# Lending more tiles to VectorE's exp, partial waves, and a normalisation that goes through DMA, in a four-layer attention kernel

## The chip, the cores and the metric

The kernel runs on one core of a Trainium2 chip. The core has TensorE (PE, matrix products into PSUM), VectorE (DVE), ScalarE (ACT), GpSimd (POOL), SyncE (SP, which issues the DMAs here), an on-chip SBUF of 128 partitions and a PSUM of eight banks of 512 float columns. The metric is the device time of one execution in microseconds, median over the runs of one kernel; the median of the kernel before is 1751.68 us.

## The reference

Four attention layers run on one sequence of 2048 tokens with 512 features and 32 heads of 16. Layers 0 and 2 are of kind A, layers 1 and 3 of kind B, each with a residual:

```python
x = x + _A_ref(_layernorm(x), A_wq, A_wk, A_wv, A_wo, A_beta)
x = x + _B_ref(_layernorm(x), B_wqkv, B_wo)
x = x + _A_ref(_layernorm(x), A_wq, A_wk, A_wv, A_wo, A_beta)
x = x + _B_ref(_layernorm(x), B_wqkv, B_wo)
```

Kind A works on four segments of 512 tokens: causal attention within the segment, plus a linear memory, mixed by a gate per head:

```python
a_dot = softmax(qs @ ks.T * scale + mask) @ vs
num   = phi(qs) @ M
den   = phi(qs) @ z + 1e-6
o     = g * (num / den) + (1.0 - g) * a_dot
M, z  = M + phi(ks).T @ vs, z + sum(phi(ks))
```

with `g = sigmoid(beta)` and `phi(t) = t + 1` for `t > 0`, else `exp(t)`. Kind B is plain full attention, softmax(q kᵀ / 4) v over all 2048 tokens. In B every head needs 2048 x 2048 exps, in A about half of 512 x 512 for each segment.

## The kernel before

The program is written by a planner. `Builder` runs through the work once in Python, with a clock for each engine that it estimates itself (`Sched.t`), and each engine's list of instructions comes out in the order in which the planner emitted them. Semaphores join the lists. A table, `PIECES`, changes the planner's settings at given times of its clock.

The work is cut into *groups*: one layer, one segment of 512 queries, four heads (chunk `c` of eight heads, `e` the even or odd ones). A group of kind B has 64 *banks*: scores of 128 keys against 512 queries for one head, 512 columns of one PSUM bank. The whole kernel has 4,864 banks. In each step (`unit`) TensorE computes the scores of two or three banks with 32-row matmuls, four of which run side by side, and ScalarE takes the exp of all of them in one instruction into `pT` (L1707). Two or three units later TensorE multiplies the exps by V (`pv`) into the accumulating bank `ACC`. V carries a seventeenth column of ones for each head, so the product also holds the sum of the exps. For full groups of B, and all groups of layer 3, the product has 17 rows by 512 queries (`fm`); for A and for partial groups of layer 1 it is done by 128 queries at a time, 17 columns per head.

VectorE takes part of the exps off ScalarE. `dx_first` (L1248) reads a bank or two from PSUM and writes, in integer arithmetic, the bits of an approximate exp into a *slot*; `dx_shift` (L1318) adds a constant to a whole slot, once for each further *chord* of the approximation, and `pool_part` (L1363) does the same on GpSimd. Each of the chords is multiplied by V on TensorE, so that such a bank costs three or four products instead of one. Slots are the tiles `dxw` (two banks each) and, once they are free, tiles of other uses that lend their space (`dx_areas`, four banks each): before, the second slots of `QA` and `VA` from the end of layer 0 until `("proj", 2, 2)`, and in layer 3 the tiles that nothing needs any more. `dx_room` decides whether a bank may go to VectorE, from how far VectorE's planned clock runs ahead of the next unit.

When a group's last product is done, `finish` normalises it. For full groups of B (`finish_fm`) VectorE transposes the 128x512 sums in 32x32 blocks (L1840), inverts the sums of exps (L1843), multiplies (L1846), and after the pair `e = 0, 1` transposes back into `oT` (L1868), from which the output projection reads. For A the inverse is also multiplied by the gate `gout` (L1816). All else (layer norm, projections, the memory, the output projection) is done by *tasks*, which the planner fits between units. While TensorE would idle, `keep_busy` gives it products with a tile of zeros. SP issues the DMAs in order, and each waits there for its semaphores: loads, stores, and the 128x512 transposes of `xT`, `oT`, `phk` and `phq`.

Of the kernel before, what the change touches and what calls it, by code (L numbers as in the profile page):

```python
# [3 lines left out]
dt = mybir.dt  # L4
# [3 lines left out]
P = 128  # L8
# [23 lines left out]
class Op:  # L32
    __slots__ = ("eng", "idx", "fn", "deps", "emit", "evno", "is_dma", "batch", "name", "end", "ghost", "ready")
# [48 lines left out]
class Sched:  # L82
# [80 lines left out]

    def add(self, eng, fn, reads=(), writes=(), deps=(), name="", banks=(), ns=300, gap=None, tile=None, extra=None):
# [9 lines left out]
        for (bk, mode, alloc) in banks:  # L174
            if mode == "w":
                if bk.alloc != alloc:
                    tail = bk.writes[-1:] + list(bk.reads.values())
# [20 lines left out]
        wit = {}  # L198
        for w in [d for g in dep_ops if g.ghost for d in g.deps] + dep_ops:
            if w.eng == "pe" and eng == "pe" and not w.is_dma:  # L200
                continue
            if w.is_dma:
                wit[("dma", id(w.batch))] = w
                continue
            cur = wit.get(w.eng)
            if cur is None or cur.idx < w.idx:
                wit[w.eng] = w
        for w in wit.values():
            if not w.is_dma:
                w.emit = True  # L210
        op.deps = list(wit.values())
        if eng == "pe" and extra is None and self.idle is not None:
            ready = max([d.end + LAG[d.eng] for d in op.deps if d.eng != "pe"], default=0.0)
            if name != "fill" and self.last:
                self.settle(ready)
            if ready > self.t["pe"] + 312:
                self.idle(ready, banks)
                op.idx = len(self.ops[eng])
                self.owed = 0
            elif self.owed and tile[0] == 128:  # L220
                self.idle(self.t["pe"], banks, self.owed)
                op.idx = len(self.ops[eng])
                self.owed = 0
        if extra is not None:
# [72 lines left out]
class Group:  # L297


    __slots__ = ("L", "kind", "qseg", "c", "e", "ksegs", "first", "last", "banks", "pos", "qm", "acc", "npv", "idx", "total", "started", "left", "taken", "shut", "fm")  # L300

    def __init__(self, L, kind, qseg, c, e, ksegs, first=True, last=True):
# [16 lines left out]
        self.idx = c * 2 + e  # L319
# [8 lines left out]
class Builder:  # L328
    NPU, NDX, FIT, MARGIN, PART, FILL_DVE, EARLY, FILL = 4, 5, 2, 450, 1, 300, 700, 0.5
# [7 lines left out]
    QREST, CLOSE, FM, NAREA, XDX, NEAR_S, NEAR_E, DX_WAIT = 24, ('proj', 2, 2), 3, 18, 99, 60, 60, 400  # L337
# [4 lines left out]
    PIECES = [(0.0, {'MIX': 0, 'OPART': 4}),  # L342
              (20.0, {'EVAC_ACT': -300, 'LOW': 32, 'DXA_REST': 14}),
              (60.0, {'CR_W': 1900, 'AHEAD': 500, 'LOW': 24, 'DXA_REST': 10, 'wide': True}),
              (100.0, {'DQ': 1900, 'wide': True}),
              (140.0, {'EVAC_ACT': 0, 'CR_W': 1400, 'AHEAD': 300, 'DX_T': 480, 'DQ': 2200}),
              (180.0, {'DX_FIN': 2500, 'PE_B': 5, 'PE_LOW': 5, 'DMA_LATE': 300}),
              (220.0, {'DX_FIN': 2000, 'PE_B': 4, 'PE_LOW': 6, 'LOW': 16, 'DX_T': 430, 'PVN': 6, 'DMA_LATE': 600}),
              (260.0, {'LOW': 24, 'NEAR_N': 200, 'PVN': 4, 'HOR': 100, 'DX_RES': 2}),
              (300.0, {'MARGIN': 700}),  # L350
              (340.0, {'FILLS': 1, 'DQ': 1900, 'DMA_LATE': 300, 'NEAR_E': 80}),
              (380.0, {'DX_T': 330, 'DQ': 2500, 'DMA_STEPS': 3, 'NEAR_E': 0, 'PSH_N': 16, 'PSH_E': 1}),
              (420.0, {'NEAR': 6}),
              (460.0, {'NEAR': 10, 'TAKEN': 1.5, 'ALTA': (1, 9, 9, 9), 'PSH': 1}),
              (480.0, {'REST': 14, 'REST_N': 20, 'PSH_E': 0, 'PSH_B': 6}),
# [623 lines left out]
    def task_B(self, L, s):  # L979
        ks = self.kslot(L, s)  # L980
        need = [("x", L, s)]
        if L == 3:
# [3 lines left out]
            if s == 2:  # L986
                need.append(("closed", self.CLOSE))
# [1102 lines left out]
```

## Time and profile before

| what | value |
|---|---|
| median of 3 runs | 1751.68 us (1751.64 to 1751.69) |
| span of the profiled execution, which is the only time given of it | 1749.6 us |
| ScalarE busy | 1708.2 us, 98% |
| TensorE busy | 1638.0 us, 94% (modelled ends) |
| VectorE busy | 1489.3 us, 85% |
| GpSimd busy | 650.2 us, 37% |
| DMA | 30.10 MB, 17 GB/s |

A row of a view of groups gives the line, the engine, the operation, the tile written and the tiles read, the shape and the count; then busy time in us, the mean duration in ns, and the engine's idle time just before such instructions with what ended it. The matmuls overlap, and so do the tails of neighbouring instructions on VectorE and ScalarE: count times mean is more than busy time.

### The profile page before, as it was taken

To read this page: it belongs to the slowest core of one execution; us is meant where nothing else is said; L and a number is where in the kernel's file an instruction comes from. 1 tells how busy PE (TensorE), PEld (TensorE's weight loads), DVE (VectorE), ACT (ScalarE), POOL (GpSimd) and SP (SyncE) were. 2 spreads that over 40 slices of the span, in tenths; PEclk is the share of its full clock that TensorE was granted. 3 is DMA by queue.
4 is the path that set the end of the run, shared out by engine and by line. 5 is a ranking of instruction groups with operands and counts; after the bars stand their busy time and mean duration, and the time that the engine had idled before them with its cause. 6 is when DMAs were issued, how large, how long until landed. Compare 5 with 4: busy or idle time off the path is not lost.

```text
span 1749.6 us, 44053 instructions
## 1 busy us (share of the span) xinstructions
PE 1638.0 (94%) x17651; PEld 574.8 (33%) x17651; DVE 1489.3 (85%) x2912; ACT 1708.2 (98%) x1662; POOL 650.2 (37%) x1204
## 2 busy tenths in 40 slices
PE   8989999999998999999999999999999999999998
PEld 4445454563224222233222332242222222222222
DVE  6677767589996999897999779767999999999997
ACT  7999999999999999999999999999999999999998
POOL 4632415110016212224221252151155556766665
PEclk9999999999999999999999999999999999999999
DMA  6121101000001000000001011010000000000000
GB/s 176 21 46 32 32 17 26 14 12 5 13 1 26 1 1 13 14 19 7 14 10 22 7 23 16 13 26 13 1 13 1 2 7 8 1 1 13 1 1 13
DMA packets 86189, 30.10 MB, mean 17 GB/s; under 512 B 78816, under 2 KB 85472, under 8 KB 85984
## 3 DMA queue, kind: packets, MB, share of 16 engines
q1 hardware_dynamic: 85984, 27.29, 7.5%
q8 instruction: 138, 2.26, 0.6%
q14 instruction: 67, 0.55, 0.1%
HBM read 6.30 MB, written 2.10 MB: 5 GB/s over the span
## 4 chain that ended last, share of the span: by engine, by line
ACT 45%; PE 30%; issue 13%; DVE 7%; POOL 2%; DMA 1%; SPq 0%; ACTq 0%; DVEq 0%; POOLq 0%
ACT pT L1707 44%; PE ps L563 30%; POOL pT L1722 2%; ACT amem L821 1%; DMA xT<-xn 1%; DVE KB L1248 1%; DVE dxw L1248 1%; DVE QA L1248 1%; DMA phk<-KA 0%; DVE xT L1248 0%; DVE dxw L1318 0%; DVE KA L1840 0%; DVE amem L946 0%; DVE VB L1248 0%; DVE VB L601 0%
## 5 line engine op out<-in xcount | busy, mean ns | idle before, releaser
L1707 ACT ACTIVATE pT<-ps 128x1024 bf16<-128x1024 f32 (+4 forms) x1612 | 1676.6, 1186 | 26.6 <-PE ps L563 19.7
L563 PE MATMUL ps<-qm,KB 32*128 32x512 bf16 x3584 | 526.0, 384 | 52.5 <-ACT pT L1707 39.0
L563 PE MATMUL ps<-pT,VB 128*17 128x512 bf16 x2187 | 371.5, 384 | 5.6 <-ACT pT L1707 2.3
L1722 POOL TENSOR_SCALAR_AFFINE_SELECT pT<-pT 128x256 bf16<-128x256 bf16 (+2 forms) x523 | 211.8, 416 | 220.7 <-ACT pT L1707 208.0
L563 PEld LDWEIGHTS ps<-qm,KB 32*128 32x128 bf16 x3584 | 134.0, 91 | 448.2 <-ACT pT L1707 336.8
L1363 POOL TENSOR_TENSOR dxw<-dxw,dxc 128x256 int32<-128x256 int32 (+1 forms) x127 | 77.7, 614 | 389.6 <-DVE dxw L1248 64.7
L563 PEld LDWEIGHTS ps<-pT,VB 128*17 128x17 bf16 x2187 | 86.6, 87 | 232.0 <-issue 199.2
L1248 DVE TENSOR_SCALAR dxw<-ps 128x512 uint16<-128x512 f32 (+1 forms) x232 | 158.5, 697 | 4.4 <-PE ps L563 3.2
L1617 POOL TENSOR_SCALAR qm<-QB,par 128x512 bf16<-128x512 bf16 x88 | 67.7, 776 | 245.6 <-PE ps L563 220.7
L1248 DVE TENSOR_SCALAR QA<-ps 128x512 uint16<-128x512 f32 (+1 forms) x170 | 120.7, 729 | 3.3 <-PE ps L563 2.8
L563 PE MATMUL ps<-qm,QA 32*128 32x512 bf16 x512 | 113.2, 384 | 8.9 <-ACT pT L1707 5.9
L563 PE MATMUL ps<-qm,KA 32*128 32x384 bf16 (+3 forms) x1024 | 101.8, 303 | 16.9 <-ACT pT L1707 13.1
L563 PE MATMUL ps<-dxw,VW 128*17 128x512 bf16 x472 | 117.5, 381 | 0.0
L563 PE MATMUL ps<-VA,pT 128*128 128x51 bf16 (+1 forms) x2560 | 105.6, 187 | 10.3 <-POOL pT L1722 6.5
L1248 DVE TENSOR_SCALAR VA<-ps 128x512 uint16<-128x512 f32 (+1 forms) x149 | 107.1, 733 | 4.4 <-PE ps L563 3.4
L1318 DVE TENSOR_SCALAR dxw<-dxw 128x1024 uint16<-128x1024 uint16 (+1 forms) x261 | 105.5, 414 | 3.4 <-PE ps L563 1.1
L563 PEld LDWEIGHTS ps<-VA,pT 128*128 128x128 bf16 x2560 | 83.7, 96 | 58.2 <-POOL pT L1722 26.1
L1248 DVE TENSOR_SCALAR KB<-ps 128x512 uint16<-128x512 f32 (+1 forms) x122 | 93.9, 787 | 4.5 <-PE ps L563 3.8
L563 PE MATMUL ps<-wB,zero 128*128 128x512 bf16 x271 | 90.4, 383 | 0.0
L563 PE MATMUL ps<-dxw,VB 128*17 128x512 bf16 x297 | 89.5, 382 | 0.1
L1248 DVE TENSOR_SCALAR VB<-ps 128x512 uint16<-128x512 f32 (+1 forms) x106 | 82.7, 794 | 3.6 <-PE ps L563 2.7
L563 PE MATMUL ps<-xT,wA 128*128 128x512 bf16 (+1 forms) x273 | 76.2, 381 | 1.3 <-DVE xT L782 0.9
(343 smaller groups left out, 2844.3 us busy)
## 6 DMA issues: line engine op xcount, KB each, us to landing
out_dram<-x SPq DMA_DIRECT2D x8, 256.0 KB, 2.1
x<-in_A_x_dram SPq DMA_DIRECT2D x3, 512.0 KB, 5.1
wB<-in_B_wqkv_dram SPq DMA_DIRECT2D x1, 1536.0 KB, 11.7
xT<-xn SPq DMA_TRANSPOSE x60, 2.4
oT<-ob SPq DMA_TRANSPOSE x36, 2.4
x<-in_A_x_dram SPq DMA_DIRECT2D x4, 128.0 KB, 2.4
wA<-in_A_wq_dram SPq DMA_DIRECT2D x1, 512.0 KB, 4.7
wA<-in_A_wk_dram SPq DMA_DIRECT2D x1, 512.0 KB, 5.8
```

Of the source, the lines that this page charges most:

```text
L563: self.sc.add("pe", lambda e: e.matmul(out, lhsT, rhs, start=start, stop=stop, skip_group_check=True), reads=reads, banks=[(bank, "w", all ...
L821: self.op("act", lambda e: e.activation(et, src, ACT.Exp), reads=bsrc, writes=self.b_amem, ns=1023, gap=915)
L1248: self.sc.add("dve", lambda e: e.tensor_scalar(d, o, SCALE * LOG2E * 128, W_C if dxs[0][:3] in self.wt else EXP_C, op0=ALU.mult, op1=ALU.add),
L1318: self.op("dve", lambda e: e.tensor_scalar(o, w, d, None, op0=ALU.add), reads=self.b_dxw[b0][:len(ents)], writes=wr, ns=(295, 425, 560, 69 ...
L1363: self.sc.add("pool", lambda e: e.tensor_tensor(o, w, c, ALU.add), reads=self.b_dxw[src][i0:i0 + n] + [self.b_dxc], writes=wr, deps=[sync] ...
L1617: self.op(eng, (lambda m, q, col: lambda e: e.tensor_scalar(m, q, col, 0.0, op0=ALU.mult, op1=ALU.add))(m, q, col), reads=[bq, self.b_par] ...
L1707: self.sc.add("act", (lambda dst, src: lambda e: e.activation(dst, src, ACT.Exp, scale=SCALE))(dst, src), writes=self.b_pT[slot * 3 + i:sl ...
L1722: self.op("pool", (lambda blk, pat: lambda e: e.affine_select(blk, blk, pattern=pat, compare_op=ALU.is_ge, fill=0.0, base=0, channel_multi ...
```

## The change

*More lenders.* `dx_areas` lists more tiles. In layer 0 the slots 2 and 3 of `KB`, `VB` and `QB` lend halves (two banks each) from the end of segment 0 until their own segment of layer 0 is done; `KB`, `VB` 4 and 5 and `QB` 0 to 2 lend in layer 2; `QB` 0 to 2 lend again in layer 3. A lender with an end is closed before the projection that writes it (`task_B` waits for `("closed", ...)`). `dxw` has four slots instead of five.

*Partial waves.* `early_parts` and `split_early` may start a pair of a B group with those key segments that are there, if the scores ahead are few (`EARLY_R`); the sums go to a free place (`accS`, slots 8 and up) and the rest of the group adds to them.

*Normalisation.* A full group's sums are only copied (or added) from PSUM to a tile `fin`. `den_rows` moves the sums of exps by DMA into a 128x32 tile `den`, VectorE inverts that once for a pair, `row` and `inv` bring the inverses through DRAM to a 128x512 tile, and GpSimd multiplies into `oT` (`run_norms`). The very last pair goes the old way.

*Gate.* V's ones column of A holds `1 + exp(beta)` instead of 1, so the sum of exps comes out already divided by `1 - g`; the product with `gout` goes, and the memory's denominator is adjusted with `gden`.

*Table.* `PIECES` is new, and `side` lets some small operations go to GpSimd where a setting says so. In the program that results none does: every `xn`, `Mn`, `Mz` and `oT<-oT,phq` still stands on VectorE.

```diff
-    NPU, NDX, FIT, MARGIN, PART, FILL_DVE, EARLY, FILL = 4, 5, 2, 450, 1, 300, 700, 0.5
+    NPU, NDX, FIT, MARGIN, PART, FILL_DVE, EARLY, FILL = 4, 4, 2, 450, 1, 300, 700, 0.5
...
-    PIECES = [(0.0, {'MIX': 0, 'OPART': 4}),
-              (20.0, {'EVAC_ACT': -300, 'LOW': 32, 'DXA_REST': 14}),
+    PIECES = [(0, {'MIX': 0, 'OPART': 4}),
+              (20, {'CR_LOW': 1500, 'DQ': 1900, 'PAIRS2': 0, 'DXS': 2, 'EVAC_ACT': -300, 'LOW': 32}),
...
+    def moves(self, pairs, reads, writes, key, ns=2450):
+
+        t = self.tsems[self.ring("tsem", 8)]
+        b, last = DmaBatch(t[0], t[1]), [t[2]] if t[2] is not None else []
+        for out, in_ in pairs:
+            t[1] += 16
+            t[2] = self.sc.add_dma("sp", (lambda out, in_: lambda e: e.dma_start(out, in_))(out, in_), b, reads=reads, writes=writes, deps=last, ns=ns,
+                                   gap=self.MOVE)
...
+        on = bcast(g[:, 0:1], [[0, 8], [1, H]])
+        self.op("dve", lambda e: e.tensor_copy(va[:, :, :, 16], on), reads=[self.b_gone], writes=[b for l in self.b_VA for b in l], ns=430)
...
+        for s in self.EARLY_S:
+            for t, b in ((self.KB, self.b_KB), (self.VB, self.b_VB), (self.QB, self.b_QB)):
+                add(t[:, s, :, :], b[s], ("attn", 0, 0), until=("attn", 0, s), halves=True)
+        for ks, s in ((4, 0), (5, 1))[:self.MORE]:
+            add(self.KB[:, ks, :, :], self.b_KB[ks], ("acc", 1), until=("attn", 2, s))
+            add(self.VB[:, ks, :, :], self.b_VB[ks], ("attn", 1, 0), until=("attn", 2, s))
+        for s in range(3 if self.MORE else 0):
+            add(self.QB[:, s, :, :], self.b_QB[s], ("attn", 1, s), until=("attn", 2, s))
...
+        for s in range(3 if self.MORE else 0):
+            add(self.QB[:, s, :, :], self.b_QB[s], ("attn", 3, s))
...
+            if pair is None and self.EARLY_Q and sum(len(g.banks) - g.pos for g in self.sel) <= self.EARLY_R:
+                pair = self.split_early()
...
+            if rows:
+                d = self.fin[g.e]
+                self.op("dve", lambda e: e.tensor_copy(d, acc), writes=self.b_fin[g.e] + new, bank=bank, alloc=g.acc, ns=690)
...
-            om = bcast(self.gout[:, h:h + 1], [[0, 4], [2, 4]])
-            r4 = rd.rearrange("p (t r) -> p t r", r=4)
-            self.op("dve", lambda e: e.tensor_tensor(r4, r4, om, ALU.mult), reads=[br, self.b_gout], writes=[br], ns=160)
...
+    def den_rows(self, g):
+
+        f, bf, c = self.fin[g.e], self.b_fin[g.e], self.den[:, :]
+        key = g.L, g.qseg, g.c
+        at = lambda a, o, dims: bass.AP(tensor=a.tensor, offset=a.offset + o, ap=dims)
+        w = f.ap[0][0]
+        self.moves([(at(c, 16 * g.e, [[32, P], [1, 16]]), at(f, 16 * w, [[32 * w, 4], [16, 32], [1, 16]]))], [bf[1]], [self.b_den[g.e]], ("den",) + key)
+        if g.e:
+            self.moves([(self.fin[0][32 * r + 16:32 * r + 32, :], f[32 * r:32 * r + 16, :]) for r in range(4)], [bf[0]], [self.b_fin[0][1]], ("fin",) + key)
+            self.norms.append([0, g])
+
+    def run_norms(self, now):
+
+        while self.norms:
+            stage, g = self.norms[0]
+            key = g.L, g.qseg, g.c
+            if not now and not self.met([("dma", ("inv" if stage else "den",) + key)]):
+                return
+            c = self.den[:, :]
+            if not stage:
+                self.op("dve", lambda e: e.reciprocal(c, c), reads=self.b_den, writes=self.b_den, ns=351)
+                at = lambda a, o, dims: bass.AP(tensor=a.tensor, offset=a.offset + o, ap=dims)
+                self.moves([(at(self.row, 512 * e, [[1024, 4], [16, 32], [1, 16]]), at(c, 16 * e, [[32, P], [1, 16]])) for e in range(2)], self.b_den,
+                           self.b_row, ("row",) + key)
+                self.moves([(self.inv[:, :], at(self.row, 0, [[512, 8], [0, 16], [1, 512]]))], self.b_row, [self.b_inv], ("inv",) + key, 3500)
+                self.norms[0][0] = 1
+                continue
+            self.norms.pop(0)
+            self.own(g)
+            o, f, v = self.oT[:, 1, g.c, :], self.fin[0], self.inv[:, :]
+            ns = (690, 1045)[self.INV_P]
+            op = self.op(("dve", "pool")[self.INV_P], lambda e: e.tensor_tensor(o, f, v, ALU.mult), reads=self.b_fin[0] + [self.b_inv],
+                         writes=[self.b_oT[1][g.c]], ns=ns)
```

How the lists change, at three places. On ScalarE in the last third of the program, where layer 2 ends and layer 3 runs, `pT<-ps` are the exps; 1536 columns are three banks, 1024 two. Before:

```order
L1707 ACTIVATE pT<-ps 128x1536
L1707 ACTIVATE pT<-ps 128x1024 x3
L1707 ACTIVATE pT<-ps 128x1536
L1707 ACTIVATE pT<-ps 128x1024 x2
L1707 ACTIVATE pT<-ps 128x1536 x2
```

and now:

```order
L1828 ACTIVATE pT<-ps 128x1024 x4
L1828 ACTIVATE pT<-ps 128x1536
L1828 ACTIVATE pT<-ps 128x1024 x10
L1828 ACTIVATE pT<-ps 128x1536
L1828 ACTIVATE pT<-ps 128x1024 x18
```

Nearly every unit there now leaves one or two of its banks to VectorE.

On VectorE in layer 3, at the end of a full group with `e = 1` (`KA` holds the tiles `tk`, `of` and now `fin`; the `TENSOR_SCALAR ...<-ps` are first exp steps, those of 2048 columns are later steps on a lent tile). Before:

```order
L1840 STREAM_TRANSPOSE KA<-ps 128x512
L1843 RECIPROCAL rd<-KA 128x16
L1846 TENSOR_TENSOR KA<-KA,rd 128x16x16
L1248 TENSOR_SCALAR xT<-ps 128x512
L1248 TENSOR_SCALAR phq<-ps 128x512
L1868 STREAM_TRANSPOSE oT<-KA 128x512
```

and now:

```order
L1922 COPY KA<-ps 128x512
L1325 TENSOR_SCALAR KA<-ps 128x512
L1325 TENSOR_SCALAR VA<-ps 128x1024
L1325 TENSOR_SCALAR VA<-ps 128x512 x2
L1977 RECIPROCAL den<-den 128x32
```

The two transposes and the product are gone; the reciprocal stands some exp steps behind the copy and waits for a DMA.

On SP during layer 1, with the tasks of layer 2 beside it. Before, only transposes stand there:

```order
L608 DMA_TRANSPOSE oT<-ob 128x4x128
L608 DMA_TRANSPOSE phk<-KA 128x4x128 x4
L608 DMA_TRANSPOSE oT<-ob 128x4x128 x3
L608 DMA_TRANSPOSE xT<-xn 128x4x128 x8
L608 DMA_TRANSPOSE oT<-ob 128x4x128
```

and now:

```order
L650 DMA den<-KA 128x1x16
L640 DMA_TRANSPOSE xT<-xn 128x4x128 x4
L650 DMA den<-KA 128x1x16
L650 DMA KA<-KA 16x512 x4
L650 DMA row<-den 4x32x16 x2
L650 DMA inv<-row 128x1x512
L640 DMA_TRANSPOSE xT<-xn 128x4x128 x4
```

The chain of a pair stands between two sets of transposes of normalised x; the second set can be issued only after `inv`, which waits for `row`.

More of the change, by code (lines that the diff above doesn't have):

```diff
@@ L223, in add @@
                 self.owed = 0
+        for w in op.deps:
+            if not w.is_dma:
+                w.emit = True
         if extra is not None:
```

421 lines of the change are left out of this document (261 added, 160 removed).

## The prediction

> **What bounds the kernel now.** I read the head of the page first, then the chain of waits, ScalarE's waits, and the busy time by stretch.
>
> ```profile
> span 1749.6 us, 44053 instructions
> PE 1638.0 (94%) x17651; PEld 574.8 (33%) x17651; DVE 1489.3 (85%) x2912; ACT 1708.2 (98%) x1662; POOL 650.2 (37%) x1204
> ACT 45%; PE 30%; issue 13%; DVE 7%; POOL 2%; DMA 1%; SPq 0%; ACTq 0%; DVEq 0%; POOLq 0%
> L1707 ACT ACTIVATE pT<-ps 128x1024 bf16<-128x1024 f32 (+4 forms) x1612 | 1676.6, 1186 | 26.6 <-PE ps L563 19.7
> ```
>
> ScalarE works 1708.2 of 1749.6 us, and 1676.6 us of that is one line, the exp of the scores (L1707). It idles 41.4 us in all, 26.6 of them before an exp. The chain alternates between ScalarE and TensorE, but that is a loop: TensorE waits for a bank that ScalarE must empty.
>
> ```profile
> 400.00:500.00 100.00, 96.25 (x843) 26.56 (x841) 97.77 (x192) 100.00 (x100) 7.70 (x11) 1.00 0.04 8
> 0.00:400.00 400.00, 369.02 (x5691) 201.39 (x5691) 286.12 (x677) 378.93 (x372) 134.98 (x322) 1.00 0.19 41
> 400.00:1350.00 950.00, 900.09 (x8490) 281.62 (x8488) 829.59 (x1665) 940.35 (x930) 267.25 (x525) 1.00 0.06 12
> 1350.00:1740.00 390.00, 363.35 (x3442) 90.41 (x3438) 369.80 (x561) 385.71 (x359) 248.00 (x358) 1.00 0.01 4
> ```
>
> Columns: stretch, its length, busy time (and instructions) of PE, weight load, DVE, ACT and POOL, then the granted clock. Of the 41.4 us of idle ScalarE, 21.1 lie in the first 400 us (loads and the first layer), 9.7 in the next 950 and 4.3 in the last 390. So the time is ScalarE's list of exps, and an edit is worth what it takes off that list. VectorE does some exps in its place. It has room early (286 of 400 us) and hardly any in the last layer (369.8 of 390).
>
> **The change on ScalarE.** I counted the instructions of both orders; the prices are these rows.
>
> ```profile
> L1707 ACT ACTIVATE pT<-ps 128x1024 bf16<-128x1024 f32 x873 | 855.9, 1079 | 8.8 <-PE ps L563 7.5 <-POOL pT L1722 0.6
> L1707 ACT ACTIVATE pT<-ps 128x1536 bf16<-128x1536 f32 x580 | 834.3, 1497 | 14.4 <-PE ps L563 10.0 <-POOL pT L1722 1.6 <-POOL qm L1617 0.3
> L599 ACT ACTIVATE KB<-ps 128x512 bf16<-128x512 f32 x3 | 1.9, 617 | 0.0
> ```
>
> Exps of 1536 columns go from 580 to 429, of 1024 from 873 to 1074; of the small ones, 512 wide go from 27 to 4, 2x256 from 28 to 8, 3x256 from 48 to 58, 256 from 56 to 66. That is 1,864,192 columns in 1612 instructions before and 1,826,304 in 1639 after: 37,888 columns, 74 score banks of 512, have left ScalarE. Two rows differ by 512 columns and 1497 - 1079 = 418 ns, so the columns save 74 x 0.418 = 30.9 us. At 0.418 us per 512, all columns of before are 1521.9 of the 1676.6 us; the other 154.7 us over 1612 instructions are 0.096 us each, and 27 more cost 2.6 us. Evacuations on ScalarE rise by 5: 5 x 0.6 = 3.0 us. Sum: -30.9 + 2.6 + 3.0 = **-25.3 us**.
>
> **The change on VectorE.** It must take the 74 banks.
>
> ```profile
> L1248 DVE TENSOR_SCALAR dxw<-ps 128x512 uint16<-128x512 f32 x226 | 151.2, 683 | 3.7 <-PE ps L563 2.6 <-POOL dxw L1363 0.4
> L1248 DVE TENSOR_SCALAR KB<-ps 128x1024 uint16<-128x1024 f32 x24 | 29.2, 1218 | 1.5 <-PE ps L563 1.0 <-POOL VB L1363 0.3
> L1318 DVE TENSOR_SCALAR dxw<-dxw 128x1024 uint16<-128x1024 uint16 x221 | 94.5, 436 | 2.9 <-PE ps L563 1.1 <-DVE QA L1248 0.2
> L1318 DVE TENSOR_SCALAR VA<-VA 128x2048 uint16<-128x2048 uint16 x47 | 32.6, 695 | 0.2 <-PE ps L563 0.2
> L1840 DVE STREAM_TRANSPOSE KA<-ps 128x512 f32<-128x512 f32 x47 | 33.2, 707 | 4.9 <-PE ps L563 4.6
> L1843 DVE RECIPROCAL rd<-KA 128x16 f32<-128x16 f32 x55 | 14.0, 254 | 1.9
> L1846 DVE TENSOR_TENSOR KA<-KA,rd 128x256 bf16<-128x256 f32 x55 | 23.4, 426 | 1.9
> L1868 DVE STREAM_TRANSPOSE oT<-KA 128x512 bf16<-128x512 bf16 x27 | 19.0, 703 | 0.2
> L1816 DVE TENSOR_TENSOR rd<-rd,gout 128x16 f32<-128x16 f32 x64 | 13.9, 217 | 2.2
> L1798 DVE COPY KB<-ps 128x512 f32<-128x512 f32 x4 | 2.7, 681 | 0.1
> L933 DVE RECIPROCAL rg<-rg 128x128 f32<-128x128 f32 x6 | 5.7, 953 | 0.2
> L1800 DVE TENSOR_TENSOR KB<-KB,ps 128x272 f32<-128x272 f32 x12 | 5.2, 431 | 0.6 <-PE ps L563 0.3
> ```
>
> First exp steps (L1248): 30 more of 512 and 22 more of 1024, 30 x 0.683 + 22 x 1.218 = +47.3. Later steps (L1318): 103 fewer of 1024 (-44.9), 49 more of 2048 (+34.1), 19 new of 1536, put halfway between 0.436 and 0.695 (+10.8): about 0. That is what the lent tiles buy: four banks go through one step at 0.174 us each instead of two at 0.218. The normalisation: 54 fewer each of the transpose, reciprocal and product, 54 x (0.707 + 0.254 + 0.426) = -74.9; 27 fewer output transposes, -19.0; 64 gate products, -13.9. In their place 40 copies of 0.681 (+27.2), 4 fewer 512-wide adds (-2.7), and 24 reciprocals of 32 columns, between the 254 ns of 16 and the 953 of 128, by width 0.35 each (+8.5). The partial waves add six copies, adds, reciprocals and products, 6 x (0.431 + 0.431 + 0.254 + 0.426) = +9.3; 5 fewer evacuations are -3.4. Sum: **-21 us** on an engine that had 260 us of idle. Over the kernel VectorE hides its work; where it may not is the first rival.
>
> **GpSimd and TensorE** stay under cover.
>
> ```profile
> L1363 POOL TENSOR_TENSOR dxw<-dxw,dxc 128x256 int32<-128x256 int32 x126 | 76.7, 611 | 388.2 <-DVE dxw L1248 64.7 <-PE ps L563 60.3 <-DVE xn L755 40.4
> L1363 POOL TENSOR_TENSOR VB<-KB,dxc 128x512 int32<-128x512 int32 x5 | 5.2, 1037 | 4.0 <-DVE KA L1846 1.5 <-PE ps L563 1.3 <-DVE VB L1318 0.6
> L563 PE MATMUL ps<-wB,zero 128*128 128x512 bf16 x271 | 90.4, 383 | 0.0
> L563 PE MATMUL ps<-pT,VB 128*17 128x512 bf16 x2187 | 371.5, 384 | 5.6 <-ACT pT L1707 2.3
> L563 PE MATMUL ps<-VB,pT 128*128 128x51 bf16 x1454 | 65.8, 187 | 0.1
> ```
>
> GpSimd gets 72 steps of 256 (+44.0), 15 of 512 (+15.6) and the 24 float products of 128x512; the nearest row, the integer add of that size, makes these 24 x 1.037 = +24.9. Some 650 + 85 = 735 us is 43% of the new span; without cover a late product would hold the next pair's sums, which come only after another 64 banks.
>
> TensorE loses 60 idle-time matmuls on zeros (60 x 90.4/271 = -20.0) and 450 products of probabilities and V in the 17-row form (at most 450 x 371.5/2187 = -76.4, at least 0 where they overlap others), and gains 2412 of the narrow form (2412 x 65.8/1454 = +109). It stays between +13 and +89 us busy, against 111.6 us idle plus the zeros that are left. The clock row reads 1.00 in the last 390 us too, where few zeros run, so fewer cost no clock.
>
> **The DMA chain.** Each of 24 pairs now sends, on SP's one queue, two `den`, four `KA<-KA`, two `row` and one `inv` (219 DMAs more with three extra transposes); `row` waits for VectorE's reciprocal and `inv` for `row`, with transposes of the next rows of x behind them.
>
> ```profile
> xT<-xn SPq DMA_TRANSPOSE x60, 2.4
> x<-in_A_x_dram SPq DMA_DIRECT2D x4, 128.0 KB, 2.4
> x<-in_A_x_dram SPq DMA_DIRECT2D x3, 512.0 KB, 5.1
> out_dram<-x SPq DMA_DIRECT2D x8, 256.0 KB, 2.1
> ```
>
> No row has these forms. From 2.1 us for a write to DRAM and between 2.4 and 5.1 us for the 256 KB of `inv`, the three hops are 6.6 to 9.6 us, with reciprocal and product 8 to 11. Cover: a pair's 128 banks take 128 x 390/1264 = 39 us in the last layer (1,264 is what its 1271 score matmuls in 390 us come to). I take the chain at nothing on the path.
>
> The Trainium skill, "DMA: Bandwidth & Descriptors", "Why a DMA increments its semaphore by 16 and not by 1", speaks against it: a DMA is spread over the largest number of engines up to 16 that divides the slowest dimension on both sides, which is 4 for `den` and `row` and 8 for `inv`. With that page's roughly 2 us fixed and 27 GiB/s per engine, `inv` would be about 3.1 us by my estimate, inside the bounds above; the sum stays as it is.
>
> **The sum.** 1749.6 - 25.3 = 1724.3 us if ScalarE's idle time stays. It may grow in the last layer. There (the last 1,264 banks by the orders) ScalarE's banks go from 849 to 817 and its exps from 363 to 390, which is 32 x 0.418 - 27 x 0.096 = 10.8 us of the gain. VectorE's list there gets about 7 us longer by the rows above: 369.8 + 7 = 376.8 us of work for a stretch of 390 - 10.8 = 379.2. The fullest window quoted has VectorE 97.77% busy; at that the stretch takes 385.4, and 6.2 us of the gain is lost. Nothing is lost if the denser list overlaps more: the 226 steps of 683 ns in the first row of VectorE make 154.4 us and cover only 151.2, since neighbours overlap. Between 0 and 6.2 I take 3.5, since the window had few GpSimd steps. Span: 1728. The runs lie 1751.7 - 1749.6 = 2.1 us above the span: **1730 us**, own range 1724 to 1737.
>
> **Rivals.** (1) VectorE becomes the bound in the last layer. For it: 95% busy there, and the same step takes different times depending on what runs beside it:
>
> ```profile
> L1318 DVE TENSOR_SCALAR dxw<-woA 128x1024 uint16<-128x1024 uint16 x4 | 1.7, 418 | 0.0
> L1318 DVE TENSOR_SCALAR dxw<-phk 128x1024 uint16<-128x1024 uint16 x6 | 3.0, 503 | 0.0
> ```
>
> If its 376.8 us must keep today's 94.8% share (369.8 of 390), the stretch takes 397.5 instead of 379.2 and the end is 1749.6 - 25.3 + 18.3 + 2.1 = 1745; range 1737 to 1748. Against it: a bank goes to VectorE only while its planned backlog is below a limit (`dx_room`), as before, and ScalarE then idled 4.3 us in 390.
>
> The Trainium skill, "SBUF — State Buffer", "SBUF: two separate sides", says that VectorE's fast two-port steps and GpSimd's work share a port pair, and whichever comes second waits for the whole instruction. The 85 ns between these two rows agree. By that rule the added GpSimd work makes this rival likelier.
>
> (2) The DMA chain costs time: VectorE's reciprocal stands in its list where the plan (2.45 us per hop) has the data landed. If `den` lands 1.3 us later than that and each of the 24 stalls reaches ScalarE, 31 us are lost: 1726.4 + 31 = 1757, slower; it decides from 1.2 us on. Against: the planned figure is already at the 2.4 us rows, VectorE has slack outside the last layer.
>
> (3) The early gain isn't delivered: partial waves and early lenders fill a list that is short of score work, ScalarE waits more in the first 400 us (21.1 idle now), and only the last layer is worth something: about 1751, no change.
>
> (4) Better: the partial waves close half of those 21.1 us: 1717 to 1723.
>
> **Chances.** Forecast 0.64, (1) 0.20, (2) 0.04, (3) 0.05, (4) 0.07. The range 1721 to 1744 leaves out (2), (3), some of (1) and (4). A measurement tells 0.2%, 3.5 us, from no change: faster 0.91, same 0.05, slower 0.04.
>
> **What would show it.** Right: L1707's counterpart near 1648 us, ScalarE's idle time 38 to 50 us, VectorE near 1470 busy and above 96% in the last layer, DMA waits of VectorE and PE of a few us in all. Wrong: ScalarE's idle time above 60 us. If it stands ahead of exps in the last layer with VectorE's first steps named by TensorE's waits, it is (1); with `den` as the releaser, (2); in the first 400 us, (3).

## The result, and the profile after

| | before | after |
|---|---|---|
| median of the runs | 1751.66 us (4 runs, 1751.25 to 1751.69) | 1736.42 us (4 runs, 1733.77 to 1738.21) |
| ratio, 95% interval | | 0.9911 (0.9897 to 0.9925) |
| profiled execution: span | 1749.6 us | 1732.0 us |

The change is faster by 15.2 us, 0.9%. The forecast was 1730 us with the range 1721 to 1744. Four more runs of the same kernel, with the experiments below, gave 1735.96 us and a ratio of 0.9901 (0.9881 to 0.9922). From the page of the changed kernel:

```profile
span 1732.0 us, 48101 instructions
PE 1596.1 (92%) x19355; PEld 625.5 (36%) x19553; DVE 1476.5 (85%) x2761; ACT 1681.6 (97%) x1694; POOL 742.4 (43%) x1317
ACT 40%; PE 27%; DVE 16%; issue 12%; POOL 2%; DMA 2%; SPq 0%; ACTq 0%; DVEq 0%; POOLq 0%
L1828 ACT ACTIVATE pT<-ps 128x1024 bf16<-128x1024 f32 (+3 forms) x1639 | 1648.7, 1154 | 37.1 <-PE ps L595 32.4
L1988 POOL TENSOR_TENSOR oT<-KA,inv 128x512 bf16<-128x512 f32 x24 | 32.7, 1362 | 114.2 <-DMA inv<-row 75.2
```

ScalarE's busy time fell from 1708.2 to 1681.6 us, by 26.6, where 25.3 were forecast; its exps (now L1828) take 1648.7 us. Its idle time rose from 41.4 to 1732.0 - 1681.6 = 50.4 us. So 26.6 us were gained and 9.0 given back: 17.6 us of span in these two executions. VectorE's share of the chain of waits went from 7% to 16%.

Where the 9 us lie is read from the busy time by stretch (columns as in the prediction; the fifth number is ScalarE). Before:

```profile
400.00:1230.00 830.00, 788.30 (x7521) 252.72 (x7518) 717.99 (x1473) 821.33 (x822) 218.97 (x454) 1.00 0.07 13
1230.00:1350.00 120.00, 111.80 (x969) 28.90 (x970) 111.60 (x193) 119.02 (x110) 48.28 (x71) 1.00 0.02 6
1350.00:1700.00 350.00, 326.79 (x3069) 81.20 (x3065) 333.41 (x509) 345.75 (x321) 220.05 (x319) 1.00 0.01 4
```

After:

```profile
0.00:400.00 400.00, 362.78 (x5938) 209.92 (x6009) 294.74 (x696) 380.23 (x378) 129.26 (x316) 0.99 0.19 40
400.00:1230.00 830.00, 767.11 (x8977) 294.36 (x9082) 701.14 (x1374) 818.14 (x818) 275.50 (x534) 1.00 0.10 19
1230.00:1350.00 120.00, 106.26 (x1002) 28.64 (x1010) 108.79 (x174) 113.33 (x119) 80.52 (x118) 1.00 0.09 25
1350.00:1700.00 350.00, 334.33 (x3228) 85.25 (x3240) 346.61 (x482) 344.78 (x359) 248.67 (x342) 1.00 0.06 16
```

ScalarE's idle time is 19.8 us in the first 400 us (21.1 before), 11.9 from 400 to 1230 (8.7), 6.7 from 1230 to 1350 (1.0) and 5.2 from 1350 to 1700 (4.3), although VectorE is 99% busy there. What grew most is the start of the last layer, not its bulk. One gap makes most of it. TensorE and ScalarE at that place, as start, duration, instruction and wait:

```profile
1333.88 1.04 PE L595 MATMUL ps<-woB,oT 128*128 128x512 bf16 x4
1335.78 1.04 PE L595 MATMUL ps<-woB,oT 128*128 128x512 bf16 x4 [0.86 <-DVE x L1102]
1337.60 1.04 PE L595 MATMUL ps<-woB,oT 128*128 128x512 bf16 x4 [0.78 <-DVE x L1102]
```

```profile
1339.06 1.02 ACT L1828 ACTIVATE pT<-ps 128x1024 bf16<-128x1024 f32 x1 [4.30 <-PE ps L595]
1340.71 1.02 ACT L1828 ACTIVATE pT<-ps 128x1024 bf16<-128x1024 f32 x1 [0.63 <-PE ps L595]
```

These matmuls are the output projection of segment 0, three of its four tiles in one row, without a score between them, each waiting for VectorE to empty the one bank they share. The planner put them there in `own`: a pair's product may be written to `oT` only when the segment that still owns that place has been projected, and the next pair's end (`run_norms(True)` in `finish`) asked for the product at once. That is read from the code and these rows; no run moves the projection.

### The profile page after: what moved, and what is told of

It reads as the page before. It is cut to its first block, busy times and chain, and to the rows that moved or that the text cites. A ratio compares the mean times of both kernels' runs of the same rounds, so it can differ in the third digit from the quotient of the medians.

```text
span 1732.0 us, 48101 instructions
## 1 busy us (share of the span) xinstructions
PE 1596.1 (92%) x19355; PEld 625.5 (36%) x19553; DVE 1476.5 (85%) x2761; ACT 1681.6 (97%) x1694; POOL 742.4 (43%) x1317
## 4 chain that ended last, share of the span: by engine, by line
ACT 40%; PE 27%; DVE 16%; issue 12%; POOL 2%; DMA 2%; SPq 0%; ACTq 0%; DVEq 0%; POOLq 0%
ACT pT L1828 39%; PE ps L595 27%; POOL pT L1843 2%; DVE QB L1325 2%; DVE VB L1325 1%; DMA phq<-amem 1%; DVE QA L1325 1%; DVE KB L1325 1%; DVE VA L1325 1%; DVE dxw L1395 1%; DVE QB L1395 1%; DVE dxw L1325 1%; DVE xT L1325 1%; ACT amem L883 1%; DVE amem L1009 1%
## 5 line engine op out<-in xcount | busy, mean ns | idle before, releaser
L1828 ACT ACTIVATE pT<-ps 128x1024 bf16<-128x1024 f32 (+3 forms) x1639 | 1648.7, 1154 | 37.1 <-PE ps L595 32.4
L595 PE MATMUL ps<-pT,VB 128*17 128x512 bf16 x1883 | 336.2, 385 | 10.4 <-ACT pT L1828 2.7
L1325 DVE TENSOR_SCALAR QB<-ps 128x512 uint16<-128x512 f32 (+1 forms) x177 | 129.4, 751 | 3.5 <-PE ps L595 3.0
L1325 DVE TENSOR_SCALAR VB<-ps 128x512 uint16<-128x512 f32 (+1 forms) x168 | 122.6, 749 | 5.5 <-PE ps L595 3.8
L595 PE MATMUL ps<-VB,pT 128*128 128x51 bf16 (+1 forms) x2892 | 117.4, 186 | 3.6 <-ACT pT L1828 1.7
L595 PE MATMUL ps<-qm,KA 32*128 32x256 bf16 (+3 forms) x1024 | 103.4, 304 | 16.9 <-ACT pT L1828 12.2
L595 PEld LDWEIGHTS ps<-VB,pT 128*128 128x128 bf16 x2892 | 94.0, 96 | 53.4 <-issue 31.6
L1325 DVE TENSOR_SCALAR dxw<-ps 128x512 uint16<-128x512 f32 (+1 forms) x116 | 82.1, 720 | 8.3 <-PE ps L595 7.7
L1988 POOL TENSOR_TENSOR oT<-KA,inv 128x512 bf16<-128x512 f32 x24 | 32.7, 1362 | 114.2 <-DMA inv<-row 75.2
L595 PE MATMUL ps<-pT,VA 128*17 128x512 bf16 x321 | 74.3, 384 | 3.6 <-DVE KA L1931 2.3
L1325 DVE TENSOR_SCALAR QA<-ps 128x512 uint16<-128x512 f32 (+1 forms) x101 | 72.2, 735 | 3.8 <-PE ps L595 3.5
```

What stands on the lines that cost most here:

```text
L595: self.sc.add("pe", lambda e: e.matmul(out, lhsT, rhs, start=start, stop=stop, skip_group_check=True), reads=reads, banks=[(bank, "w", all ...
L1325: self.sc.add("dve", lambda e: e.tensor_scalar(d, o, SCALE * LOG2E * 128, W_C if dxs[0][:3] in self.wt else EXP_C, op0=ALU.mult, op1=ALU.add),
L1828: self.sc.add("act", (lambda dst, src: lambda e: e.activation(dst, src, ACT.Exp, scale=SCALE))(dst, src), writes=self.b_pT[slot * 3 + i:sl ...
L1988: op = self.op(("dve", "pool")[self.INV_P], lambda e: e.tensor_tensor(o, f, v, ALU.mult), reads=self.b_fin[0] + [self.b_inv], writes=[self ...
```

## The experiments

Except for the one with the old table, each kernel below keeps the planned order of the changed kernel and is edited after planning, since the planner makes another order of everything if one cost differs. Places are compared by the end of the same ScalarE instruction in two traces (each has 1,690 activations, in the same order). The trace that they are compared with is the second one of the changed kernel, its fastest run: 1728.3 us, 5.4 us under the mean of its eight.

**The changed kernel again, and needless work in the last layer.** Edits, inserted at even distances in the engine's list from about 1350 to 1695 us:

```diff
+ act: e.activation(M_as_bf16[:, 0:512], self.wB[:, 0, 0:512], ACT.Exp, scale=SCALE)     # x24
+ dve: e.reciprocal(bet_as_f32[:, 0:16], self.gtok[:, 0:16])                              # x48
```

> The changed kernel once more, with a second trace. Both theories: 1733 to 1738 us. If the extra waits are a property of the plan, the four largest idle gaps of ScalarE outside the start (4.3 us near 1339, 3.1 near 84, 1.6 near 308, 1.0 near 585) return at the same places within 0.3 us. If they are chance (a transfer, the clock), they move or vanish, and the records with a granted clock below 1 stand at other times than 92, 320 and 744 us.

> 24 needless exps of 128x512 on ScalarE, spread over the last layer (about 1350 to 1695 us); everything else is as in the changed kernel. By the row spacing of such exps, 0.49 us each, this is 11.8 us. Theory (ScalarE's list sets the time): +11 to +12 us. Rival (VectorE has become the bound there): ScalarE's idle time of some 5 us in the stretch absorbs part, +6 to +8 us.

> 48 needless reciprocals of 128x16 on VectorE, spread over the same stretch of the last layer; everything else is as in the changed kernel. At 0.254 us each this is 12.2 us on an engine that is idle for some 4.5 us there. Theory (ScalarE sets the time, VectorE follows it closely): +5 to +8 us. Rival (VectorE is the bound): +11 to +13 us.

Measured: 1735.96 us for the kernel again, 1743.98 with the exps and 1737.58 with the reciprocals. From 1340 us to the end the exps cost 9.4 us and the reciprocals at most 2.7 us: 1.1 us of that fell after 1700 us, where no reciprocal stands and that trace has a record of half clock (TensorE had half its clock for 3.41 us, from 1706.9 us). In the same stretch, with 24 exps more and with 48 reciprocals more:

```profile
1350.00:1700.00 350.00, 322.63 (x3134) 80.84 (x3146) 339.35 (x469) 346.98 (x372) 242.91 (x334) 1.00 0.06 15
```

```profile
1350.00:1700.00 350.00, 334.86 (x3212) 86.17 (x3217) 347.48 (x528) 344.01 (x357) 248.17 (x340) 1.00 0.06 16
```

VectorE around one of the reciprocals:

```profile
1406.39 0.68 DVE L1325 TENSOR_SCALAR xT<-ps 128x512 uint16<-128x512 f32 x1
1406.99 0.23 DVE L2224 RECIPROCAL bet<-gtok 128x16 f32<-128x16 f32 x1
1407.15 1.15 DVE L1325 TENSOR_SCALAR xT<-ps 128x1024 uint16<-128x1024 f32 x1
```

An exp takes 0.52 us from its start to the next one's, 12.6 us for the 24 (11.8 were estimated); some three quarters of it came through. By the medians it is 8.0 us, the upper end of the rival's range, so this run alone does not decide. The reciprocals do: a record lasts 237 ns (11.4 us for the 48), but the next instruction starts 159 ns after it (7.6 us), and at most 2.7 of these 7.6 us came through, less than either expected, though the engine was 99% busy and its busy time grew by only 0.9 us (346.61 to 347.48) in the 350. The busy share counts the records of instructions that overlap, by nearly 80 ns at each end here, and it says 99% before the engine is full. ScalarE's list sets the time; VectorE was not the bound.

In the second trace the 4.30 us gap returned (at 1335.6 us), as did those near 84 (1.9 us), 308 (2.2) and 584 (0.9). So these waits belong to the plan, but for the two early ones the size changes. The 4.30 us stand ahead of the same exp in every kernel below that keeps the planned order. The records with a lower clock moved: one instead of three.

**The DMA chain.** Two transfers of 16 KB between DRAM tensors ahead of each `inv`, one after the other, and then one:

```diff
  row   <- den
+ hop0  <- row          # two kernels: with hop0 alone, with hop0 and hop1
+ hop1  <- hop0
  inv   <- row          # now waits for the last hop
```

> Two more transfers of 16 KB between DRAM tensors ahead of each of the 24 transfers into inv, one after the other, so that each chain from denominators to product gets two hops of some 2 us longer, about 4 us in all; everything else is as in the changed kernel. Theory (the chain is off the path): within 1.5 us of the changed kernel. Rival (the chain is on the path): 24 x 4 = +96 us, or, if only the four pairs that follow the one before them by 16 to 21 us are tight, +4 to +16 us.

Measured: 1796.63 us, 61 us more than the changed kernel, far from the theory and on neither of the rival's figures. My reason for taking the chain at nothing, that a pair's banks cover it, fell. The reciprocal-to-product time went from 7.4 to 10.9 us (means of the 24), so 3.5 us of delay cost 2.5 us per pair on average, unevenly: 27.1 us of it lie between 1230 and 1340 us. The waits of that kernel (who waited for whom: us, times, longest), and TensorE and GpSimd at one place:

```profile
POOL oT L1991 <- DMA inv<-row: 126.2, 14, 58.5
DVE KA L1934 <- POOL oT L1991: 23.0, 5, 6.2
PEld ps L596 <- DVE KA L1934: 26.2, 12, 6.0
```

```profile
1441.86 1.26 POOL L1991 TENSOR_TENSOR oT<-KA,inv 128x512 bf16<-128x512 f32 x1 [4.04 <-DMA inv<-row]
1443.08 2.38 POOL L1443 TENSOR_TENSOR KB<-QA,dxc 128x256 int32<-128x256 int32 x3
```

```profile
1444.19 0.60 PE L596 MATMUL ps<-KB,wA 128*17 128x512 bf16 x1 [3.34 <-POOL KB L1443]
1444.72 0.61 PE L596 MATMUL ps<-qm,KB 32*128 32x512 bf16 x3
```

Two mechanisms show. The next pair's first sum on VectorE (L1934 here) writes the tile that the product reads, so it waits for the product. And GpSimd works in order: exp steps stand behind the late product, TensorE behind the exp steps, and the score matmuls behind that then take 0.61 us instead of 0.39, at half the clock. The mean clock fell to 0.977 in these runs; what part of the cost is the clock's, no run separates. The transposes that wait behind the chain in SP's queue are not the cost: the waits of VectorE, ScalarE and TensorE for any DMA come to 17.4 us in that trace, against 12.3 in the second trace of the changed kernel. How much room the chain has is seen in the second trace of the changed kernel, VectorE at two places:

```profile
1232.91 0.69 DVE L1931 TENSOR_TENSOR KA<-KB,ps 128x512 f32<-128x512 f32 x1 [0.19 <-PE ps L595]
1236.56 0.34 DVE L1977 RECIPROCAL den<-den 128x32 f32<-128x32 f32 x1
1244.73 0.69 DVE L1931 TENSOR_TENSOR KA<-KB,ps 128x512 f32<-128x512 f32 x1 [1.44 <-POOL oT L1988]
...
1458.74 0.68 DVE L1922 COPY KA<-ps 128x512 f32<-128x512 f32 x1
1462.80 0.34 DVE L1977 RECIPROCAL den<-den 128x32 f32<-128x32 f32 x1
1477.29 0.68 DVE L1922 COPY KA<-ps 128x512 f32<-128x512 f32 x1
```

A pair's last sum, its reciprocal, the next pair's first sum. In the last ten pairs 17 to 20 us lie between these sums; the product (1470.84 to 1472.11 us here) ends 3.8 to 8.1 us before the next sum. In the five pairs from 1230 to 1340 us the rest that partial waves left is short, the next sum follows after 11 to 13 us, and the product ends 0.03 to 0.9 us before it: no room at all. The next kernels test these two claims, the room and the two mechanisms. One moves products later in GpSimd's list, one gives every second pair of the last layer another tile for its first sum:

```diff
+ pool[k:j + 1] = pool[k + 1:j + 1] + [product]          # x_late 3.5 us, x_hop_late 7 us of planned time
...
+ def first(self, g): return ob_as_f32 if g.L == 3 and g.c % 2 else self.fin[0]
+ sum_of_pair.all = [... without the product of the pair before, with that of two pairs before]
```

> One more hop in each chain instead of two, about 1.8 us. Theory (the cost begins where the room ends: none in five pairs from 1230 to 1340 us, some 4 to 6 us ahead of the next sum in the last ten): 2 to 3.5 us in each of the five and 0 to 8 us in the others, +10 to +25 us, 1746 to 1761 us. Rival (the cost is proportional to the delay, as a queue that all else waits in would make it): +31 us, 1767 us.

Measured with one hop: 1748.91 us, +13. Against the second trace of the changed kernel it is 2.2 us behind at 1230 us, 16.7 at 1365 and 15.9 at the end: 0.8 us in the 670 us before (2.2 less the 1.4 it had at 560 us), 14.5 us in six pairs, nothing in the last nine. The hop takes 2.0 us from issue to landing. In the five close pairs the chain got 0.9 to 2.5 us longer, and each next sum started 0.03 us after the product's end. One hop eats nearly the whole gain of the change. The cost begins where the room ends.

> The same second buffer, with the two more hops in each chain. Theory (two mechanisms: the next sum waits for the late product, and GpSimd stands in order at the late product with exp steps behind it; VectorE waited 23.0 us for products): 15 to 28 us of the +61 us go, 1768 to 1782 us, nearly all of it between 1230 and 1340 us. Rival (all of it is GpSimd's standing): 1792 to 1800 us.

Measured: 1783.43 us, 13.2 us less than with two hops alone, a little under the range expected. It lost 15.1 us from 1230 to 1340 us instead of 27.1. VectorE's wait for products is gone from its waits; GpSimd's for `inv` stands at 126.2 us as before (19.1 in the second trace of the changed kernel). So the shared tile is shown, with 12 of 27 us in the close pairs. That GpSimd's standing costs the rest is argued from its waits: no run takes it away.

> In the last layer the sums of every second pair go to another buffer (the tile ob, unused there), so that the next pair's first sum no longer waits for the product of the pair before; the order of all instructions stays. In the second trace of the changed kernel three of these sums stood 1.44, 1.02 and 0.13 us behind the product (1244 to 1336 us), two more came within 0.9 us of it. Theory (the partial waves bring pairs so close that the chain has no room there, and this costs a little in the changed kernel already): 1 to 4 us better, median 1732 to 1735 us. Rival (what VectorE waits there is slack): within 1 us of the changed kernel.

Measured: 1734.87 us (1731.36 to 1737.58). That is 1.1 to 1.6 us below the changed kernel's two medians, and no difference by their spread. From 1230 to 1400 us it is 0.5 us faster than the second trace of the changed kernel and 1.4 us faster than the first. The product is on the edge in the changed kernel: VectorE's two waits for it (1.44 and 1.02 us) cost little or nothing, and no kernel here is clearly faster than the changed one.

> Each of the 24 GpSimd products moved behind those of the next GpSimd instructions that do not need it, up to 3.5 us of planned time later (none in three pairs, one to seven instructions in the others, 0.6 us in four of the five pairs from 1230 to 1340 us); nothing else moves. Theory (the product stands where inv is planned to land, and the changed kernel's transfers land just in time): within 1.5 us of the changed kernel in the profiled run, and at most 2 us better in the median. Rival (the spread from run to run comes from transfers that land late now and then): the runs come together at 1730 to 1733 us.

> The kernel with two more hops in each chain, with the products moved up to 7 us of planned time later in GpSimd's list (5 to 7 us in nearly all pairs from 1350 us on and in four pairs before 1010 us; 0.6 us in the pairs from 1230 to 1290 us, where the next pair's sums need the product at once). Theory (a late transfer costs time because GpSimd waits in order, with VectorE's exp steps behind it): of the +61 us, what came after 1340 us (some 20 us) and half of the 14 us before 1010 us go, 1765 to 1778 us; what came from 1230 to 1340 us stays. Rival (the cost is in the transfers themselves, or in SP's queue): 1790 to 1800 us as without the move.

Measured: 1750.30 us for the products moved 3.5 us, 14 us worse than the changed kernel and against both expectations; 1801.63 us with two hops, 5 us worse than without the move, where the two sets of four runs overlap: no gain, where 1765 to 1778 us were expected. In the first, from 1230 to 1365 us (12.7 us lost against the second trace):

```profile
DVE KA L1931 <- POOL oT L1988: 9.8, 5, 2.0
PEld ps L595 <- DVE KA L1931: 13.6, 12, 3.4
```

From 1365 us on it lost only some 3 us. Its profiled run is the longest of its ten, 25 us behind the second trace; of the 9.6 us lost before 1230 us, 5.2 lie at 1015 us, where TensorE's output projection waits for the moved product:

```profile
1015.39 0.61 PE L595 MATMUL ps<-woB,oT 128*128 128x512 bf16 x1 [3.61 <-POOL oT L1988]
```

With the hops and a 7 us move the product starts 13 to 16 us after the reciprocal in the last ten pairs, so that it ends when the next sum is already due, and VectorE waits at the copies of the last pairs (L1925) as well:

```profile
DVE KA L1934 <- POOL oT L1991: 24.6, 5, 6.6
DVE KA L1925 <- POOL oT L1991: 12.7, 7, 2.5
```

So a product is bound on both sides: earlier, GpSimd stands at `inv`; later, VectorE stands at the tile, or TensorE at `oT`.

**The clock.** A trace records the share of its clock that TensorE was granted; the mean of each run is listed with its span:

| kernel, runs | mean span | mean clock |
|---|---|---|
| before, 55 | 1750.0 us | 0.9988 |
| changed, 8 | 1733.7 us | 0.9966 |
| products later, 10 | 1748.8 us | 0.9925 |

In the first trace of the changed kernel, the stretches of 3.4 us ahead of and in its three records of half clock:

```profile
76.90:80.30 3.40, 1.69 (x28) 0.96 (x26) 2.85 (x10) 3.40 (x4) 2.38 (x7) 1.00 0.00 0
80.30:83.70 3.40, 3.40 (x21) 1.64 (x19) 1.08 (x3) 0.31 (x1) 0.73 (x2) 0.51 0.57 116
305.60:309.00 3.40, 1.48 (x33) 1.12 (x30) 2.06 (x4) 1.82 (x4) 0.74 (x2) 1.00 0.35 69
309.00:312.40 3.40, 3.40 (x20) 0.89 (x19) 1.36 (x3) 3.33 (x3) 1.98 (x7) 0.51 0.25 52
728.90:732.30 3.40, 2.27 (x39) 0.99 (x34) 2.48 (x5) 3.40 (x4) 1.04 (x3) 1.00 0.03 5
732.30:735.70 3.40, 2.93 (x25) 0.65 (x27) 2.98 (x7) 2.59 (x4) 2.25 (x4) 0.50 0.19 39
```

TensorE was busy for 1.69, 1.48 and 2.27 of 3.40 us, and at 0.51 of its clock in the stretch after. The records start 67 and 124 times 3.413 us apart, and the second trace has its one at 306.9 us: a fixed grid that lies differently in every run, so that the same weak place is hit in one run and missed in the next. The Trainium skill, "TensorE: Matmul & The Clock Gate", section "What's actually happening", says the same: a free-running window of 3413 ns decides, and does not restart with the kernel. Busy time alone does not decide here: on the same grid TensorE is busy for 1.93 us from 1336.46 to 1339.87 us of the first trace, and full clock follows. A line through the eight runs of the changed kernel rises 1.4 us for each 0.001 of clock, one through 27 of before 1.0 us. Two kernels test whether the zeros hold the clock:

```diff
- ADD = 0.6
+ ADD = 0.8                                  # x_zero: 23 zeros more, and 6 + 6 by hand ahead of 80 and 309 us
...
+ op.ghost = op.ghost or op.name in ("fill", "add")      # x_nozero: none of the 211
```

> 35 more matmuls on zeros where TensorE waits by the plan: six each in the two waits ahead of the half-clock records at 80 and 309 us, and 23 more in single waits over the whole kernel (the limit ADD goes from 0.6 to 0.8, which moves no other instruction). Theory (the changed kernel has fewer zeros, so TensorE's clock is halved for 3.4 us now and then, and a run is longer by some 1.5 us for each such record): mean clock 0.998 to 1.000 in all runs instead of 0.995 to 0.997, median 1731 to 1734 us, and the two gaps of ScalarE at 84 and 308 us (4.7 us together in the changed kernel, 4.1 in its second trace) below 2.5 us together. Rival (the clock has no part in it): clock records and time as in the changed kernel, 1735 to 1738 us.

> The changed kernel without any of its 211 matmuls on zeros; they change no result, and the order of all else stays. In the runs of both kernels so far a run is longer by 1.0 to 1.4 us for each 0.001 that its mean clock is lower. Theory (the zeros keep TensorE's clock up, so 60 fewer of them cost the changed kernel some of its clock): mean clock below 0.990 and, at 1.4 us for each 0.001, 10 us or more above the changed kernel, 1745 us or more. Rival (the clock falls for another reason, such as the phase of its window, and the zeros have no part): clock 0.995 to 0.998, within 2 us of the changed kernel, 1734 to 1738 us.

Measured without zeros: 1748.92 us, mean span 1746.6 us, mean clock 0.9736 (11 runs, 0.969 to 0.977). The zeros hold the clock, and 211 of them are worth 12.9 us of span, 0.06 us each on average. For a clock 0.023 lower that is 0.6 us for each 0.001, about half of what the two lines say, so the lines are not a price of the clock alone. Measured with more zeros: 1742.43 us and a mean clock of 0.994, both worse, against either expectation. So 35 more zeros in these places do not help, and that the 60 zeros which the change took out cost its clock stays an estimate. At the first place the bank was released too late, and the six zeros ran after the wait, at full clock:

```profile
78.44 0.59 PE L596 MATMUL ps<-qm,KA 32*128 32x512 bf16 x3
80.40 1.47 PE L2227 MATMUL ps<-wB,zero 128*128 128x512 bf16 x6 [1.37 <-DVE ob L1952]
```

There they only stood in the way: ScalarE's gap near 84 us is 3.16 us, as long as with the half clock in the first trace (3.10), against 1.94 in the second trace, and the half clock came at 92 us. At 309 us the record is gone and ScalarE's gap is 1.13 us (1.58 and 2.16 in the two traces of the changed kernel). But the kernel without zeros has no record there either, so this may be where the grid lay. And 5.7 us of what was lost against the second trace fell between 830 and 960 us, where a record of 10.24 us begins after a transfer that was late for VectorE:

```profile
889.94 0.42 DVE L1088 TENSOR_TENSOR oT<-oT,phq 128x512 bf16<-128x512 bf16 x1 [1.73 <-DMA phq<-amem]
```

Whether the added zeros had a part in that, and why the mean clock was lower in these runs, is open.

**The table.** The changed code with `PIECES` of the kernel before:

> The changed code with the table of the kernel before, so that the planner makes another order of everything. By the count of its instructions ScalarE has 3,619 banks of exps instead of 3,567 and 37 fewer instructions: 52 x 0.426 - 37 x 0.064 - 6 x 0.6 = +16 us of work. Theory that the code parts bring the gain by themselves: 1750 to 1756 us, its idle time as in the changed kernel. Theory that the table and the code only work together: ScalarE idles 100 us or more beyond that, above 1840 us.

Measured: 1882.27 us, in one run. Its page:

```profile
span 1880.5 us, 48686 instructions
PE 1709.1 (91%) x19757; PEld 648.0 (34%) x19757; DVE 1461.7 (78%) x2791; ACT 1709.1 (91%) x1651; POOL 752.6 (40%) x1350
L1814 ACT ACTIVATE pT<-ps 128x1024 bf16<-128x1024 f32 (+4 forms) x1602 | 1675.8, 1165 | 112.5 <-PE ps L581 101.7
```

ScalarE works 27.5 us more than with the new table and idles 171.4 us. The new code needs its new table; the old code with the new table was not run. So taking one part of the change away and planning anew measures a bad plan and not the part; what lenders, partial waves and the new normalisation are worth each was not measured.

## Why the prediction was right, and where not

**What bounds the kernel: right.** ScalarE's list sets the time; some three quarters of the work added to it came through.

**The change on ScalarE: right.** -25.3 forecast, -26.6 measured; 1648 us of exps forecast, 1648.7 measured.

**The change on VectorE: mis-sized.** -21 forecast (its terms add up to -21.6), -12.8 measured (1489.3 to 1476.5). Summed by form, the normalisation, the copies, the partial waves and the first steps agree within 1 us. The later steps were put at 0 and are +7.9: I priced 49 more steps of 2048 at the 695 ns of the row quoted, while all of them take 706 ns on average before and 720 after; those of 1024 went from 436 to 443. The traces show where: steps of 2048 that start while GpSimd is idle take 687 ns before and 683 after, and nine that start beside one of the new float products take 1188 on average. That fits the port pair that the Trainium skill describes ("SBUF — State Buffer", "SBUF: two separate sides", cited in the prediction).

**The last layer: right in sign, too careful.** 3.5 us of idle were added (0 to 6.2); from 1350 to 1700 us it is 1.0. The share at which VectorE is full was read from its busy time, and that is not its limit: at 99%, at most 2.7 of 7.6 us came through. Rival (1) did not happen, and its premise was weak.

**GpSimd: right where it counts.** 735 us forecast, 742.4 measured. The float product takes 1362 ns, not the integer add's 1037: 7.8 us more for 24, about that difference.

**TensorE.** Its busy time can't be judged, since the trace after lacks 198 matmuls (19,355 of 19,553 weight loads). "Fewer zeros cost no clock" is the step that failed outright: the mean clock fell from 0.9988 to 0.9966, and 60 fewer at 0.06 us are 3.7 us by estimate. No run shows that these 60 are the cause; the plan's waits changed too. The step was read off the clock column of a stretch of 390 us, where 3.4 us at half clock still read 1.00.

**The DMA chain: near nothing, as far as tested, and by luck.** The wait for the shared tile costs 0.5 to 1.4 us from 1230 to 1400 us; what GpSimd's waits cost the changed kernel was not taken out. "Cover: a pair's 128 banks take 39 us" failed. The tile is wanted again after 64 banks, about 18 us, as the same prediction said under GpSimd; and a pair that a partial wave has cut is followed after 11 to 13 us. From the last sum to the end of the product the chain takes 11 to 14 us in the last layer (up to 15 before), not 8 to 11. The chain fits with nothing to spare in five pairs, and one hop of 2.0 us more costs 13 us. Rival (2) was priced at 24 equal stalls of VectorE's reciprocal and given 0.04; that wait is 1.4 us in all, once. The danger was real at another place, the product, and in five tight pairs instead of 24.

**Partial waves.** Rival (4) wanted half of 21.1 us; 1.3 us came. That they bring pairs' ends close, and so force an output projection (4.3 us) and leave the chain no room, was in no rival.

**The sum.** 1728 us of span forecast; 1732.0 and 1728.3 us in the two traces, 1733.7 us in the mean of eight runs. Against the first trace, the idle time that I did not have is 5.7 us from 1230 to 1350 us and 3.2 us from 400 to 1230 us; 2.5 us in the last layer and 1.3 us each in the first 400 us and in ScalarE's work went the other way, and 0.5 us came at the end. So errors of both signs cancel in part, and that the number came this close is partly luck. The forecast of 1730 us is 6.4 us under the median, which lies near the upper end of the forecast's own range (1724 to 1737). ScalarE's 50.4 us of idle time are just above the 38 to 50 named as a sign of being right.

## What to carry to other kernels

Take the cover of a chain from the next use of what it holds, at the closest pair of uses and not the average one; test it by making the chain a known step longer, since a chain that fits with nothing to spare looks the same as one with much room. Where an engine waits in order, look at what stands behind the wait before moving anything later or earlier. And a column that averages the clock over 400 us hides a half-speed stretch of 3.4 us: look for long matmuls, and count the zeros that hold the clock as part of the cost of whatever replaces them.

## What the runs showed of the hardware

- In the first trace of the changed kernel TensorE's clock was halved for 3.41 us after stretches of 3.4 us in which it was busy 1.5 to 2.3 us, but not after every such stretch (1.93 us at 1336 us). In other kernels the records last 3.41 us or a multiple of it (up to 10.24 us with more zeros). The grid lies differently in each run, and with it the time of the same kernel moves: eight runs of the changed kernel, 0.995 to 0.999 of clock, 1728.3 to 1736.5 us of span. The forecast had no place for such a spread, since the three runs of before lay within 0.05 us; the 55 later ones have spans of 1748.2 to 1753.6 us.
- One more transfer of 2.0 us in a chain without room cost 14.5 us over six pairs. Of eight records of half clock in that trace, five lie between 1251 and 1371 us, where the second trace of the changed kernel has none; the clock's part in the cost was not separated.
- VectorE at 99% of busy time took 48 small instructions, 7.6 us from start to next start, for at most 2.7 us.
- VectorE's 128x2048 steps took 683 ns when GpSimd was idle at their start, and 1188 on average for the nine that started beside a float product of GpSimd.
- GpSimd's float product of 128x512 into bf16 takes 1.36 us on average, against 1.04 us for the integer add of that size.
